# Layer two's second matrix product by seven block products for two of three token groups, with its output transposed

## The chip, the core and the metric

The kernel runs on one core of one Trainium2 chip. The metric is device time in microseconds (us) for one execution. TensorE multiplies matrices, VectorE, ScalarE and GpSimd work elementwise, and SyncE issues the transfers.

## The reference

A windowed attention over 4 sequences of 576 tokens gives 2304 tokens of 512 values; two feed-forward layers follow. The change touches the attention and layer one only in their order, and layer two in its second product.

```python
x = attention(q, k, v)                      # 2304 x 512, window 32, plain and dilated heads
h = x @ moe_w_in                            # layer one: 512 -> 1024
e = exp(h - max(h)); s = h * e / (sum(e) + 1e-9)
x = layernorm(s) * g_ln @ moe_w_out         # 1024 -> 512
h = x @ moe2_w_in                           # layer two: 512 -> 2048
g = h * sigmoid(1.702 * h)
out = g @ moe2_w_out                        # second product of layer two: 2048 -> 512
```

## The kernel before

Each float32 product is made as three products of rounded parts: a high part and a low part of either factor, high by high, high by low and low by high. So every operand is split first: ScalarE copies the high part, VectorE or GpSimd subtracts it to get the low part.

Layer one handles 128 tokens at a time. Attention units (`u`), layer one's first product (`h`), transposes (`lt`) and its second product (`y`) are interleaved. Layer two runs in three passes `p` of 768 tokens, each as a pair of 384-token blocks (`TB2 = 384`).

In a pass the first product already uses seven block products instead of eight (`h_prod`, m = 0 to 6, for eight quads q of two output blocks of 128 rows): six matmuls of 384 columns for each m and q. VectorE adds the results together; ScalarE and VectorE apply the sigmoid gate; the results are the tiles `g`. For each of the 16 tiles, `o_hi` (line 703) and `o_lo` (line 706) split 768 columns, and `o_prod` (line 726) makes the second product: for six groups of 128 tokens, three matmuls of 512 columns each, with the tokens as the stationary side. That is 288 matmuls of 512 columns a pass.

Layer two's weights arrive as 64-bit values. A weight unit is fetched (line 569), turned into float32 (ScalarE lines 370 and 378, VectorE lines 382 and 386), summed where the block products need sums (`unit_sum`, line 578, GpSimd or VectorE; only for the first product before), split (`unit_hi`, line 595, and `unit_lo`, line 599), and stored to DRAM. Units in `KEEP` are prepared during pass 0 and used from the room where they were split. A unit waits in one of three rooms `raw` until split. Nine rooms `hl` hold split weights; one quad of the first product needs four.

The order of work on each engine is written out by a planner in the kernel: each piece has a rank, assumed costs, room it takes and gives back, and pieces that it follows. On each engine the planner places, as its own clock advances, the first piece by rank that can start. The lists `LOADS`, `HEAD`, `HEAD2`, `PARK`, `EXP_EACH`, `LOW_DVE`, `NORM_ANY`, `LO_POOL` and `EAGER` set ranks and choices of engine.

## Time and profile before

| | us |
|---|---|
| median of 3 runs (694.85 to 695.95) | 695.17 |
| the profiled execution | 696.08 |
| its span, first to last instruction | 694.3 |
| TensorE busy in the span | 669.4 |
| VectorE busy in the span | 438.5 |
| ScalarE, GpSimd busy in the span | 346.6, 170.6 |

A group of instructions is given by line, engine, operation and tile, with its count, the busy time and the mean duration. Matmuls overlap at their ends, so the mean of one is longer than the time from one start to the next; the same holds for other engines by some tens of ns. The granted clock is a share of TensorE's full speed.

### The profile page before, as it was taken

What the parts mean: (1) busy time and instruction counts of PE and PEld (TensorE: products, weight loads), DVE (VectorE), ACT (ScalarE), POOL (GpSimd) and SP (SyncE); (2) the same over time, 40 slices, a digit from 0 to 9 for tenths busy, and PEclk for the clock granted to TensorE, in tenths of its full rate; (3) what the DMA queues carried; (4) which work ended last, traced back from release to release, by engine and by line L of the source; (5) the groups of instructions that cost most, each with busy time, mean ns of one, the idle gap of its engine ahead of it and who ended that gap; (6) DMA issues with size and microseconds to landing.
All of it is one profiled execution on the core that took longest, in us unless ns stands there. A gap on an engine that the chain in (4) does not pass through costs nothing.

```text
span 694.3 us, 11999 instructions
## 1 busy us (share of the span) xinstructions
PE 669.4 (96%) x4729; PEld 597.9 (86%) x4729; DVE 438.5 (63%) x680; ACT 346.6 (50%) x676; POOL 170.6 (25%) x166
## 2 busy tenths in 40 slices
...
GB/s 281 305 307 219 65 84 189 162 138 108 115 79 64 224 178 241 251 333 71 349 250 207 163 242 244 261 262 276 247 248 123 131 113 232 273 198 96 141 128 121
DMA packets 42072, 133.99 MB, mean 193 GB/s; under 512 B 5664, under 2 KB 5664, under 8 KB 42016
## 3 DMA queue, kind: packets, MB, share of 16 engines
q1 hardware_dynamic: 42016, 133.22, 56.0%
...
q14 instruction: 19, 0.16, 0.1%
...
## 4 chain that ended last, share of the span: by engine, by line
PE 83%; DVE 10%; ACT 3%; DMA 2%; issue 1%; POOL 0%; SPq 0%; DVEq 0%; ACTq 0%
PE oa L726 18%; PE hz L661 14%; PE y L538 14%; PE h L465 12%; PE hx L661 11%; PE ob L726 9%; PE lt L516 2%; PE xt L325 2%; PE ptp L309 1%; PE s L228 1%; DVE w1r L382 1%; DVE pt L315 1%; DVE nm L473 1%; DVE wo_l L438 1%; DVE y L578 1%
## 5 line engine op out<-in xcount | busy, mean ns | idle before, releaser
L661 PE MATMUL hz<-yc,ws 128*128 128x384 f32 x576 | 108.5, 335 | 0.9 <-DVE g L678 0.9
L726 PE MATMUL oa<-w,gs 128*128 128x512 f32 x432 | 103.9, 389 | 0.0
L706 DVE TENSOR_TENSOR gs<-g,gs 128x768 fp32r<-128x768 f32 x48 | 46.3, 966 | 90.3 <-ACT gs L703 90.3
L661 PEld LDWEIGHTS hz<-yc,ws 128*128 128x128 f32 x576 | 100.4, 188 | 1.7 <-DVE g L678 1.7
L726 PEld LDWEIGHTS oa<-w,gs 128*128 128x128 f32 x432 | 81.1, 188 | 16.7
L703 ACT CAST gs<-g 128x768 fp32r<-128x768 f32 x48 | 39.9, 836 | 99.9 <-PE ob L726 98.9
L661 PE MATMUL hx<-yc,ws 128*128 128x384 f32 x432 | 82.8, 334 | 0.0
L538 PE MATMUL y<-lnh,wo_h 128*128 128x256 f32 x288 | 82.7, 287 | 0.0
L538 PE MATMUL y<-lnh,wo_l 128*128 128x256 f32 x288 | 81.5, 283 | 0.0
L538 PE MATMUL y<-lnl,wo_h 128*128 128x256 f32 x288 | 81.5, 283 | 0.0
L661 PEld LDWEIGHTS hx<-yc,ws 128*128 128x128 f32 x432 | 75.6, 188 | 0.2
L465 PE MATMUL h<-wi_h,xh 128*128 128x512 f32 x144 | 60.2, 418 | 0.0
L465 PE MATMUL h<-wi_h,xl 128*128 128x512 f32 x144 | 57.8, 402 | 0.3 <-DVE xl L454 0.3
L465 PE MATMUL h<-wi_l,xh 128*128 128x512 f32 x144 | 57.5, 400 | 0.0
L538 PEld LDWEIGHTS y<-lnh,wo_h 128*128 128x128 f32 x288 | 55.1, 191 | 0.6
L538 PEld LDWEIGHTS y<-lnl,wo_h 128*128 128x128 f32 x288 | 55.2, 192 | 0.3
L538 PEld LDWEIGHTS y<-lnh,wo_l 128*128 128x128 f32 x288 | 55.1, 191 | 0.0
L726 PE MATMUL ob<-w,gs 128*128 128x512 f32 x216 | 54.8, 389 | 0.0
L690 ACT ACTIVATE sg<-g 128x768 f32<-128x768 f32 (+1 forms) x48 | 32.7, 686 | 31.8 <-DVE g L681 27.1
L726 PEld LDWEIGHTS ob<-w,gs 128*128 128x128 f32 x216 | 40.5, 188 | 8.4
L301 POOL TENSOR_TENSOR t<-t,sx 128x768 f32<-128x768 f32 (+1 forms) x20 | 29.1, 1455 | 45.4 <-DVE sx L296 43.9
L690 ACT ACTIVATE sg<-hx 128x384 f32<-128x384 f32 x24 | 11.8, 492 | 48.8 <-PE hx L661 48.8
(333 smaller groups left out, 1203.6 us busy)
## 6 DMA issues: line engine op xcount, KB each, us to landing
...
ws<-w1d SPq DMA_DIRECT2D x48, 384.0 KB, 5.6
...
v<-in_v_dram SPq DMA_DIRECT2D x14, 384.0 KB, 3.9
...
```

The lines of the kernel that those rows point to most:

```text
L228: nc.tensor.matmul(ps[64 * par:64 * par + 64, h, wp * KW:wp * KW + KW], q_[rows, c:c + QW], k_[rows, c:c + KW], start=not masked, stop=not ...
L301: eng.tensor_tensor(t, t, wide(sms.pop(n), t.shape[1]), ALU.mult)
L309: nc.tensor.transpose(ps[:, j * P:j * P + P], t[:, 4 * h + j, :], ident)
L325: nc.tensor.matmul(ps[64 * h:64 * h + 64, w * QW:w * QW + QW], vW[4 * b + u][:, h, w, :], pt[:, h, w * QW:w * QW + QW], start=True, stop=True)
L465: nc.tensor.matmul(hps[i][:, half, :], x[:, kt, :], w[:, kt, fs], start=(kt == 0 and j == 0), stop=(kt == KT - 1 and j == 2))
L516: nc.tensor.transpose(ps[:, j, :], es[i][:, f * P:f * P + P], ident)
L538: nc.tensor.matmul(yps[g, dm][:, 0:n], w[:, f, ds_], x[:, f, 0:n], start=(f == 0 and j == 0), stop=(f == NF1 - 1 and j == 2))
L661: nc.tensor.matmul(ps[:, 0:TB2], quad_weights(q, m, kk, a), yc2[m][:, x, kk, :], start=(m < 4 and kk == 0 and i == 0), stop=(kk == 1 and i ...
L690: nc.scalar.activation(sg, src, AF.Sigmoid, scale=1.702)
L703: nc.scalar.copy(gsp[f][:, 0], gst[f])
L706: nc.vector.tensor_tensor(gsp[f][:, 1], gst.pop(f), f32(gsp[f][:, 0]), ALU.subtract)
L726: nc.tensor.matmul(acc[t2][k], gsp[f][:, x, ts_], w2[f][:, w, :], start=(f == 0 and i == 0), stop=(f == NF2 - 1 and i == 2))
```

## The change

In passes 1 and 2 the second product is made by seven block products too. Output blocks and weights change sides: weights are stationary, 384 tokens stream, and the output is written transposed (512 x 2304) and put right on the host. For each jj of eight, four products (m = 0 to 3) need three sums of `g` blocks, and for each jj three more (m = 4 to 6) follow after all jj's first four; a fourth sum is needed before m = 5. Each m and jj is six matmuls of 384 columns. The results are added together from PSUM (`o_p1`, `o_u2`, `o_u3`, `o_out`). Pass 0 keeps the eight plain block products (`o_plain`), with weights stationary: twelve matmuls of 384 columns for each jj, block and half.

The weight units of the second product now get the four sums and two splits each, and two stores. `o_load` brings two transfers of 512 KB for each jj, and `o_load2` brings pairs of 256 KB transfers in runs of 1 KB for m = 4 to 6. `KEEP` has 11 units for 12; five units of the second product are prepared with layer one, for four before. `unit_lo` may run on VectorE as well. The lists that order attention and layer one are replaced.

```diff
     def unit_fetch(u, room):
...
         a, s_ = (x.bitcast(F32).rearrange("p (c n) -> p c n", c=4) for x in words(raws[u]))
-        x, y_, op = ((a[:, 3], a[:, 2], ALU.add), (s_[:, 0], a[:, 0], ALU.subtract),
...
         if u[0] == "o":
-            x, n, d = low, 512, w2d[u[1]]
...
-            x, n, d = low[:, 0:3 * P], 3 * P, w1d[u[1]][:, 14 * P * u[2]:14 * P * u[2] + 6 * P]
-        else:
...
+            x, n, at_ = (low[:, P:], 3, 14 * u[2]) if part == 0 else (top, 4, 14 * u[2] + 6)
+        hl = hls[u, part][:, 0:2 * n * P]
+        by = hl.rearrange("p (c a n) -> p a c n", c=n, a=2)
+        return x.rearrange("p (c n) -> p c n", c=n), by[:, 0], by[:, 1], \
+            wd[u[0], u[1]][:, at_ * P:(at_ + 2 * n) * P], hl
 
     def unit_hi(u, part, hl):
...
-
-    def o_hi(p, f):
-        gsp[f] = wk2.tile([P, 2, 2 * TB2], F32R, tag="gs", name=f"gs{p}_{f}")
-        nc.scalar.copy(gsp[f][:, 0], gst[f])
-
-    def o_lo(p, f):
...
+
+    def o_block(jj, half, b):
+        return gst[jj + NQ * half][:, b * TB2:b * TB2 + TB2]
+
+    def o_sum(jj, i):
+
+        b11, b12, b21, b22 = (o_block(jj, h, b) for h in range(2) for b in range(2))
+        o, x, y_, op = ((b12, b22, b12, ALU.subtract), (b11, b12, b11, ALU.add),
+                        (b12, b22, b11, ALU.subtract), (b21, b21, b11, ALU.subtract))[i]
+        nc.vector.tensor_tensor(o, x, y_, op)
+
+    def o_hi(p, jj, m, half, b):
+        gsp[jj, m] = wk2.tile([P, 2, TB2], F32R, tag="gs", bufs=NGS, name=f"gs{p}_{jj}_{m}")
+        nc.scalar.copy(gsp[jj, m][:, 0], o_block(jj, half, b))
+
+    def o_lo(p, jj, m, half, b):
+        nc.vector.tensor_tensor(gsp[jj, m][:, 1], o_block(jj, half, b), f32(gsp[jj, m][:, 0]), ALU.subtract)
+
+    oX, oZ, ob, w2o, w2t = {}, {}, {}, {}, {}
+
+    def o_load(jj, d, hl):
+
+        w2o[jj, d] = hl
+        nc.sync.dma_start(f32(hl), wd["o", jj][:, (16 * d + 6) * P:(16 * d + 14) * P])
+
+    def o_load_all(jj, d, hl):
+
+        w2o[jj, d] = hl
+        nc.sync.dma_start(f32(hl), wd["o", jj][:, 16 * d * P:(16 * d + 8) * P])
+
+    def o_plain(jj, half, b):
+
+        first, last = seen.get(b, 0) == 0, seen.get(b, 0) == 2 * NQ - 1
+        seen[b] = seen.get(b, 0) + 1
+        if first:
+            acc[b] = [psA.tile([P, 2, 512], F32, tag="A", name=f"oa{r}") for r in range(2)] if b == 0 else \
+                [[psB.tile([P, 512], F32, tag="B", name=f"ob{r}{d}") for d in range(2)] for r in range(2)]
+        for r in range(2):
+            for d in range(2):
+                w = w2o[jj, d] if ("o", jj, d) not in KEEP else hls[("o", jj, d), 0]
+                ps = (acc[b][r][:, d] if b == 0 else acc[b][r][d])[:, 0:TB2]
+                k = ((3, 1), (0, 2))[r][half]
+                for i, (a, x) in enumerate(((0, 0), (0, 1), (1, 0))):
+                    nc.tensor.matmul(ps, w[:, (2 * k + a) * P:(2 * k + a + 1) * P], gsp[jj, 2 * half + b][:, x],
+                                     start=first and i == 0, stop=last and i == 2)
+
+    acc, seen = {}, {}
...
+    def o_load2(p, m, jj):
+
+        t = stage[0].tile([P, 2, 2, 2 * P], F32R, tag="raw", bufs=NRAW, name=f"w2_{p}_{m}_{jj}")
+        at_ = (2, 4, 14)[m - 4] * P
         for k in range(2):
-            ts_ = slice((2 * t2 + k) * P, (2 * t2 + k) * P + P)
-            for i, (x, w) in enumerate(((0, 0), (0, 1), (1, 0))):
-                nc.tensor.matmul(acc[t2][k], gsp[f][:, x, ts_], w2[f][:, w, :],
-                                 start=(f == 0 and i == 0), stop=(f == NF2 - 1 and i == 2))
-
...
+            w2t[m, jj + k] = t[:, k]
+            nc.sync.dma_start(f32(t[:, k]), wd["o", jj + k].rearrange("p (d c) -> p d c", d=2)[:, :, at_:at_ + 2 * P])
+
+    def o_prod(p, jj, m):
+        k = seen[p, m] = seen.get((p, m), 0) + 1
+        first, last = k == 1, k == NQ
+        if first and m < 2:
+            oX[m] = psA.tile([P, 2, 512], F32, tag="A", name=f"ox{p}_{m}")
+        elif first and m < 4:
+            oZ[m] = [psB.tile([P, 512], F32, tag="B", name=f"oz{p}_{m}_{d}") for d in range(2)]
+        for d in range(2):
+            ps = (oX[1 if m == 1 else 0][:, d] if m in (0, 1, 4) else oZ[2 if m in (2, 5) else 3][d])[:, 0:TB2]
+            k = (0, 2, 3, 1)[m] if m < 4 else 0
+            for i, (a, x) in enumerate(((0, 0), (0, 1), (1, 0))):
+                w = w2o[jj, d][:, (2 * k + a) * P:(2 * k + a + 1) * P] if m < 4 else w2t[m, jj][:, d, a * P:a * P + P]
+                nc.tensor.matmul(ps, w, gsp[jj, m][:, x], start=m < 4 and first and i == 0, stop=last and i == 2,
+                                 skip_group_check=True)
...
+    def o_p1(p, d):
+        hp1["o", d] = wk2.tile([P, TB2], F32, tag="p1", bufs=NP1, name=f"op{p}_{d}")
+        nc.scalar.copy(hp1["o", d], oX[0][:, d, 0:TB2])
+
+    def o_u2(p, d):
+        nc.vector.tensor_tensor(hp1["o", d], oX[1][:, d, 0:TB2], hp1["o", d], ALU.add)
...
+    def o_u3(p, d):
+        hU3["o", d] = wk2.tile([P, TB2], F32, tag="u3", name=f"ou{p}_{d}")
+        nc.vector.tensor_tensor(hU3["o", d], oZ[2][d][:, 0:TB2], hp1["o", d], ALU.add)
...
+    def o_out(p, c, d, copy=None):
+
+        if d == 0:
+            ob[c] = wk2.tile([P, 2 * TB2], F32, tag="sg", name=f"ob{p}_{c}")
+        o = ob[c][:, d * TB2:d * TB2 + TB2]
+        if c == 1:
+            copy(o, oX[0][:, d, 0:TB2])
+        else:
+            nc.vector.tensor_tensor(o, oZ[2 if c == 2 else 3][d][:, 0:TB2], (hU3 if c == 0 else hp1)["o", d], ALU.add)
+
+    def o_store(p, c):
+        r, b = ((1, 1), (0, 0), (1, 0), (0, 1))[c]
+        t = 2 * TB2 * p + TB2 * b
+        nc.sync.dma_start(out[2 * P * r:2 * P * r + 2 * P, t:t + TB2].rearrange("(d p) t -> p d t", p=P),
+                          ob[c].rearrange("p (d t) -> p d t", d=2))
...
         for n, u in enumerate(PARK[k]):
-            r = R2 + 190 + 10 * u[1] - O_AHEAD if u in KEEP else at["h", PARK_AT[k]] + PARK_STEP * n + 0.2
+            r = R2 + 190 + 20 * u[1] + u[2] - O_AHEAD if u in KEEP else at["h", PARK_AT[k]] + PARK_STEP * n + 0.2
...
-            for i in range(0 if u[0] == "o" else 4):
+            for i in range(4):
                 w = add(r, "POOL", 0.35, lambda u=u, i=i: unit_sum(u, i, nc.gpsimd), [w], port=True,
                         also=[("DVE", 0.23, lambda u=u, i=i: unit_sum(u, i, nc.vector))])
-            for part in range(1 if u[0] == "o" else 2):
-                fin = part == 1 or u[0] == "o"
...
-                    give=() if u in KEEP else (hl,))
-                if u in KEEP:
+                    give=() if u in KEEP and not fin else (hl,))
+                if u in KEEP and not fin:
...
         r0 += 200
...
-            if kept:
-                w = split_done[("o", f), 0]
-                hi_now[("o", f), 0].after.append(ready[-1])
+        lead, now, gsum = 25, {}, {}
+
+        def operand(jj, m, half, b, after, give=()):
+            w = add(r - lead, "ACT", 0.47, lambda: o_hi(p, jj, m, half, b), after, take=("gs",))
+            return add(r - lead, "DVE", 0.5, lambda: o_lo(p, jj, m, half, b), [w], port=True, give=give)
+
+        def total(jj, i, after, k=25):
+            gsum[jj, i] = add(r - k, "DVE", 0.5, lambda: o_sum(jj, i), after, port=True)
+            return gsum[jj, i]
+
+        for jj in range(NQ if p == 0 else 0):
+            r = r0 + 20 * jj
+            loads = []
...
+                def load(p=p, jj=jj, d=d):
+                    o_load_all(jj, d, hl_tile(f"wo{p}_{jj}_{d}", hi_now[p, "o", jj, d], hl_end[p, "o", jj, d]))
+                hi_now[p, "o", jj, d] = w = add(
+                    r - 60, "SP", W_T, load, [stored[("o", jj, d), 0]] + ready[-1:], take=("hl",), lag=2.0)
+                loads.append(w)
+            for b in range(2):
+                for half in range(2):
+                    op = operand(jj, 2 * half + b, half, b, muls[jj], give=("g",) if b else ())
+                    x = add(r, "PE", 2.08, lambda jj=jj, half=half, b=b: o_plain(jj, half, b),
+                            loads + [op, prods[QUADS[-1], 3]],
+                            take=(("A", "A"), ("B",) * 4)[b] if jj == half == 0 else (),
+                            give=("gs", "hl", "hl") if b and half else ("gs",))
+                    now[jj, 2 * half + b] = x
...
+        for jj in range(NQ):
+            r = r0 + 10 * jj
+            loads = []
+            for d in range(2):
+                def load(p=p, jj=jj, d=d):
+                    o_load(jj, d, hl_tile(f"wo{p}_{jj}_{d}", hi_now[p, "o", jj, d], hl_end[p, "o", jj, d]))
+                hi_now[p, "o", jj, d] = w = add(
+                    r - 60, "SP", W_T, load, [stored[("o", jj, d), 0], stored[("o", jj, d), 1]] + ready[-1:], take=("hl",),
+                    lag=2.0)
+                loads.append(w)
+            t3 = total(jj, 0, muls[jj], 50)
+            b11 = operand(jj, 0, 0, 0, muls[jj])
+            t2 = total(jj, 1, [t3, b11])
+            ops = [b11, operand(jj, 1, 0, 0, [t2]), operand(jj, 2, 0, 1, [t3])]
+            t1 = total(jj, 2, [t2, ops[2]])
+            ops.append(operand(jj, 3, 0, 1, [t1]))
+            for m in range(4):
+                x = add(r, "PE", 1.042, lambda p=p, jj=jj, m=m: o_prod(p, jj, m), loads + [ops[m], prods[QUADS[-1], 3]],
+                        take=(("A",), ("A",), ("B", "B"), ("B", "B"))[m] if jj == 0 else (),
+                        give=("gs", "hl", "hl") if m == 3 else ("gs",))
+                now[jj, m] = x
+            for d in range(2):
+                hl_end[p, "o", jj, d] = x
+        end_ = [[now[jj, m] for jj in range(NQ)] for m in range(4)]
+
+        def store(c, ws):
+            add(r, "SP", 1.3, lambda p=p, c=c: o_store(p, c), ws, give=("sg",), lag=2.0)
+
+        p1 = [add(r, "ACT", 0.45, lambda p=p, d=d: o_p1(p, d), end_[0], take=("p1",)) for d in range(2)]
+        u2 = [add(r, "DVE", 0.53, lambda p=p, d=d: o_u2(p, d), end_[1] + [p1[d]], give=("A",) if d else ()) for d in range(2)]
+        u3 = [add(r, "DVE", 0.53, lambda p=p, d=d: o_u3(p, d), end_[2] + [u2[d]], take=("u3",)) for d in range(2)]
+        c22 = []
+        for d in range(2):
+            c22.append(add(r, "DVE", 0.53, lambda p=p, d=d: o_out(p, 0, d), end_[3] + [u3[d]] + c22, give=("u3",),
+                           take=() if d else ("sg",)))
+        store(0, c22)
+        wait = {4: p1, 5: u3, 6: c22}
+        for m in (4, 5, 6):
+            xs_ = []
+            for jj in range(NQ):
+                r = r0 + 10 * (NQ * (m - 3) + jj)
+                if jj % 2 == 0:
+                    w = add(r - 60, "SP", 1.7, lambda p=p, m=m, jj=jj: o_load2(p, m, jj),
+                            [stored[("o", jj + k, d), part] for k in range(2) for d in range(2) for part in range(2)] +
+                            [now[1, 0]], take=("raw",), lag=2.0)
+                if m == 4:
+                    now["b21", jj] = op = operand(jj, m, 1, 0, muls[jj])
+                elif m == 5:
+                    t4 = total(jj, 3, [now["b21", jj], gsum[jj, 1], now[jj, 2]])
+                    t4.give = ("g",)
+                    op = operand(jj, m, 1, 0, [t4])
+                else:
+                    op = operand(jj, m, 1, 1, muls[jj] + [gsum[jj, 0], gsum[jj, 2], gsum[jj, 3]], give=("g",))
+                x = add(r, "PE", 1.042, lambda p=p, m=m, jj=jj: o_prod(p, jj, m), [w, op] + wait[m] + end_[3],
+                        give=("gs", "raw") if jj % 2 else ("gs",))
+                xs_.append(x)
+            if m == 4:
+                c = add(r, "ACT", 0.45, lambda p=p: o_out(p, 1, 0, nc.scalar.copy), xs_, take=("sg",))
+                c11 = [c, add(r, "DVE", 0.53, lambda p=p: o_out(p, 1, 1, nc.vector.tensor_copy), xs_ + [c], give=("A",))]
+                store(1, c11)
...
+                cs = []
+                for d in range(2):
+                    cs.append(add(r, "DVE", 0.53, lambda p=p, c=m - 3, d=d: o_out(p, c, d), xs_ + cs,
+                                  take=() if d else ("sg",), give=("B",) if m == 5 else ("B", "p1")))
+                store(m - 3, cs)
...
 NA = 2
 TB2 = 384
-NHL, NHL2, NRAW = 6, 3, 3
-SLOTS = {"A": 2, "B": 4, "S": 1, "qk": 2, "v": 3, "l": 1, "t": 3, "pt": 2, "ln": 4, "x": 2, "e": 3, "raw": NRAW, "hl": NHL, "p1": 2, "u3": 2, "sg": 2, "g": 16, "gs": 2,
+NQ = NF2 // 2
+NHL, NHL2, NRAW, NGS, NP1 = 6, 3, 3, 5, 4
+SLOTS = {"A": 2, "B": 4, "S": 1, "qk": 2, "v": 3, "l": 1, "t": 3, "pt": 2, "ln": 4, "x": 2, "e": 3, "raw": NRAW, "hl": NHL, "p1": NP1, "u3": 2, "sg": 2, "g": 16, "gs": NGS,
...
-LOADS = [('q', 0), ('m', 0), ('q', 2), ('q', 1), ('q', 3), ('v', 0), ('v', 1), ('w', 0), ('v', 2), ('w', 2), ('w', 1),
...
+LOADS = [('q', 0), ('m', 0), ('v', 1), ('w', 0), ('q', 3), ('q', 2), ('w', 2), ('v', 0), ('q', 1), ('w', 1), ('q', 4),
+         ('w', 3), ('q', 6), ('g', 0), ('v', 3), ('w', 5), ('w', 4), ('v', 2), ('l', 0), ('q', 5), ('v', 5), ('v', 4),
+         ('l', 1), ('v', 6), ('w', 7), ('q', 7), ('w', 6), ('v', 7), ('l', 2), ('q', 8), ('v', 8), ('q', 9), ('v', 9),
...
+HEAD = [('u', 4), ('h', 1), ('u', 3), ('u', 1), ('w', 1), ('u', 0), ('w', 2), ('u', 2), ('h', 0), ('w', 3), ('w', 0)]
+HEAD2 = [[('w', 6)], [('w', 5), ('w', 7), ('w', 4)], [], [], []]
...
-EXP_EACH = (0, 3, 4, 6, 7, 8, 9)
+EXP_EACH = (0, 2, 3, 4, 7, 9)
...
-LOW_DVE = (1, 2)
-NORM_ANY = (0, 2, 7)
+LOW_DVE = (2, 6, 7)
+NORM_ANY = (0, 3, 4, 9)
...
-LO_POOL = (0, 1)
-EAGER = {0: (4, 99), 3: (2, 99)}
+LO_POOL = (2,)
+EAGER = {3: (0, 99)}
...
-PARK = {1: [("q", 0, 0), ("q", 0, 1)],
-        2: [("q", 1, 0), ("q", 1, 1), ("q", 2, 0), ("q", 2, 1), ("q", 3, 0), ("q", 3, 1)],
-        3: [("q", 4, 0), ("q", 4, 1), ("q", 5, 0), ("q", 5, 1), ("q", 6, 0), ("q", 6, 1), ("q", 7, 0), ("q", 7, 1)] +
-        [("o", f) for f in range(16)]}
-PARK_AT = {1: 4, 2: 4, 3: 11}
-PARK_STEP = 3
+PARK = {1: [('q', 4, 1), ('q', 0, 1), ('q', 3, 1)],
+        2: [('q', 4, 0), ('q', 3, 0), ('q', 1, 0), ('q', 2, 1), ('q', 6, 0), ('q', 5, 0)],
+        3: [('q', 0, 0), ('q', 7, 1), ('q', 7, 0), ('q', 5, 1), ('q', 2, 0), ('q', 1, 1), ('o', 0, 0), ('o', 0, 1),
+            ('q', 6, 1), ('o', 1, 1), ('o', 1, 0), ('o', 2, 0), ('o', 2, 1), ('o', 3, 1), ('o', 3, 0), ('o', 4, 0),
+            ('o', 5, 0), ('o', 5, 1), ('o', 4, 1), ('o', 6, 0), ('o', 7, 1), ('o', 7, 0), ('o', 6, 1)]}
+PARK_AT = {1: 4, 2: 9, 3: 9}
+PARK_STEP = 2
 QUADS = [0, 1, 2, 3, 4, 5, 6, 7]
-KEEP = [("o", f) for f in range(4, 16)]
-O_AHEAD = 60
+KEEP = [('o', 0, 1), ('o', 1, 0), ('o', 1, 1), ('o', 2, 0), ('o', 3, 0), ('o', 3, 1), ('o', 4, 0), ('o', 5, 0),
+        ('o', 5, 1), ('o', 6, 1), ('o', 7, 1)]
+O_AHEAD = 140
...
-LOAD_AT = 5
-ULO_ANY = False
+ULO_ANY = True
 _INS = ["qk", "qk_last", "v", "v_last", "masks", "w_in", "w_out", "g_ln", "w2_in", "w2_out"]
-_OUTS = [((2304, 512), 'float32')]
+_OUTS = [((512, 2304), 'float32')]
```

## Rows read from the trace of the kernel before

**Rows 1.** The page: busy time of each engine; the chain that ended last, by engine
```profile
PE 669.4 (96%) x4729; PEld 597.9 (86%) x4729; DVE 438.5 (63%) x680; ACT 346.6 (50%) x676; POOL 170.6 (25%) x166
...
PE 83%; DVE 10%; ACT 3%; DMA 2%; issue 1%; POOL 0%; SPq 0%; DVEq 0%; ACTq 0%
```

**Rows 2.** Busy time by stage: start:end, length, engines, granted clock, DMA share, GB/s
```profile
0.00:100.00 100.00, 84.76 (x990) 69.25 (x991) 84.63 (x122) 71.81 (x152) 43.33 (x39) 0.93 0.67 212
100.00:300.00 200.00, 196.43 (x1735) 175.92 (x1733) 140.97 (x239) 131.76 (x296) 105.14 (x113) 1.00 0.48 163
300.00:375.74 75.74, 74.89 (x475) 74.57 (x474) 53.24 (x87) 37.44 (x66) 8.76 (x7) 1.00 0.67 234
375.74:442.24 66.50, 65.70 (x289) 53.89 (x289) 41.72 (x52) 32.61 (x52) 13.41 (x9) 1.00 0.65 231
442.24:500.73 58.49, 58.49 (x338) 58.24 (x337) 39.35 (x68) 21.89 (x37) 0.00 (x0) 1.00 0.76 268
500.73:566.05 65.32, 65.32 (x290) 54.05 (x289) 23.58 (x31) 17.37 (x24) 0.00 (x0) 1.00 0.42 146
...
624.54:689.88 65.34, 65.33 (x289) 53.72 (x287) 16.72 (x19) 14.52 (x19) 0.00 (x0) 1.00 0.32 112
689.88:694.30 4.42, 0.00 (x0) 0.00 (x0) 0.69 (x1) 0.00 (x0) 0.00 (x0) 0.88 0.69 255
```

**Rows 3.** VectorE in order of time at 504 us: start, duration
```profile
503.69 0.95 DVE L697 TENSOR_TENSOR g<-g,sg 128x768 f32<-128x768 f32 x1
504.56 0.55 DVE L699 TENSOR_TENSOR g<-g,sg 128x384 f32<-128x384 f32 x1
505.03 0.42 DVE L636 TENSOR_TENSOR y<-y 128x256 f32<-128x256 f32 x1
```

**Rows 4.** VectorE groups, 500 to 566 us: the next pass's inputs
```profile
L647 DVE TENSOR_TENSOR yc<-y,yc 128x512 fp32r<-128x512 f32 (+2 forms) x8 | 5.6, 716 | 0.0
...
L636 DVE TENSOR_TENSOR y<-y 128x256 f32<-128x256 f32 (+1 forms) x2 | 1.4, 684 | 0.0
...
L636 DVE TENSOR_TENSOR y<-y,y 128x512 f32<-128x512 f32 x1 | 0.7, 684 | 0.0
```

**Rows 5.** ScalarE, a copy of 384 columns
```profile
L666 ACT COPY p<-hx 128x384 f32<-128x384 f32 x24 | 11.6, 482 | 23.2 <-PE hx L661 23.2
```

**Rows 6.** VectorE, work on one weight unit and the like
```profile
L269 DVE TENSOR_TENSOR t<-s,mx 128x768 f32<-128x768 f32 x3 | 2.8, 939 | 0.1
L434 DVE TENSOR_TENSOR wi_l<-w1r,wi_h 128x1024 fp32r<-128x1024 f32 x2 | 2.4, 1201 | 0.0
...
L386 DVE SCALAR_TENSOR_TENSOR raw_('o', 14)_4875<-raw_('o', 14)_4875 128x512 uint32<-128x512 uint32 x1 | 1.8, 1802 | 0.0
...
L578 DVE TENSOR_TENSOR raw_('q', 4, 0)_2889<-raw_('q', 4, 0)_2889 128x128 f32<-128x128 f32 x4 | 1.1, 281 | 0.0
...
L382 DVE SCALAR_TENSOR_TENSOR raw_('o', 12)_4838<-raw_('o', 12)_4838 128x512 uint32<-128x512 uint32 x1 | 0.7, 693 | 1.4 <-ACT raw_('o', 12)_4838 L378 1.4
```

**Rows 7.** GpSimd, the same kinds of work
```profile
L578 POOL TENSOR_TENSOR y<-y 128x128 f32<-128x128 f32 x9 | 3.9, 459 | 1.2 <-DVE sm L484 1.0
...
L599 POOL TENSOR_TENSOR hl_('o', 10)_0_4808<-raw_('o', 10)_4747,hl_('o', 10)_0_4808 128x512 fp32r<-128x512 f32 x1 | 1.3, 1322 | 1.3 <-ACT hl_('o', 10)_0_4808 L595 1.3
```

**Rows 8.** SyncE's issues of the raw weight units, with their start
```profile
L569 SPq DMA_DIRECT2D raw_('o', 6)_4130<-in_w_out_dram x1: 372/372/372, 327.8 to 327.8; - x1
L569 SPq DMA_DIRECT2D raw_('o', 7)_4661<-in_w_out_dram x1: 333/333/333, 384.0 to 384.0; - x1
```

**Rows 9.** DMA packets: whole run, by size; then the hardware queue, 455 to 495 us and 505 to 560 us
```profile
DMA packets 42072, 133.99 MB, mean 193 GB/s; under 512 B 5664, under 2 KB 5664, under 8 KB 42016
...
q1 hardware_dynamic: 3453, 11.19, 79.3%
...
q1 hardware_dynamic: 2592, 9.05, 47.4%
```

**Rows 10.** The chain that ended last, at 99 us
```profile
98.75 3.49 DVE y L578 x4
```

146 lines of the change are left out of this document (63 added, 83 removed), and 2 rows, old and new, of the table LOADS.

## The prediction

> **What bounds the kernel now.** I read the page first, then the stages, then the groups inside the stages that change. The page and the chain of waits say TensorE: it is busy 669.4 of 694.3 us, and 83% of the chain that ended last runs through it [rows 1]. This is an average, so the stages come next [rows 2]. From 300 us on TensorE has no gaps worth naming: in pass 1 the first product fills 58.49 of 58.49 us and the second 65.32 of 65.32; pass 2's second product fills 65.33 of 65.34. What it does there sets the time one for one. The other engines have room: VectorE is busy 23.58 us in pass 1's second product, ScalarE 17.37. The first 100 us differ: TensorE is busy 84.76 us at a granted clock of 0.93, VectorE 84.63 us, and there the chain runs through VectorE, for instance 3.49 us of weight sums at 99 us [rows 10]. After the last matmul 4.42 us remain for one VectorE copy and the store.
>
> **The change part by part.**
>
> *TensorE in passes 1 and 2.* The new matmuls have the shape of the first product's: a 128x128 stationary block, 384 streamed columns, a new block for each. A first product has 8 x 7 x 6 = 336 of them in 58.49 us [rows 2], so one costs 0.174 us from start to start. The new second product has 8 jj x 7 m x 6 = 336 too, hence 58.49 us against 65.32 and 65.34: -6.83 and -6.85, together -13.7.
>
> *TensorE in pass 0.* 8 jj x 2 blocks x 2 halves x 12 = 384 matmuls x 0.174 = 66.85 us. Before, TensorE was busy 65.70 of 66.50 us there [rows 2]: +1.15, with the old gap of 0.8 kept.
>
> *The tail.* The last store is 384 KB where it was 256 KB. In the second window of [rows 9] 9.05 MB took 47.4% of 16 engines for 55 us, 417 engine-us, so 2.88 us a MB over sixteen: 0.13 MB more is 0.4. The two additions ahead of it take as long as the old copy of 0.69 us to within 0.3, since the first can run while the last three matmuls do. I take +0.4.
>
> *VectorE in pass 1.* Each jj has 7 low parts and 4 sums, all of 384 columns: 88 a pass. A busy time of 0.55 us is not the interval: the operation at 504.56 is followed by the next at 505.03, so 0.47 [rows 3]. 88 x 0.47 = 41.4; eleven additions from PSUM at 0.47 are 5.2; preparing pass 2's inputs is 5.6 + 1.4 + 0.7 = 7.7 [rows 4]. That is 54.3 of 58.49 us: full, but it fits. By halves: m = 0 to 3 last 32 x 6 x 0.174 = 33.4 us on TensorE, and VectorE has 56 x 0.47 + 7.7 = 34.0 us, of which five low parts (five rooms `gs`) and some ten sums, 7.0 us, can be done earlier in the 19.1 us that VectorE is idle in the first product [rows 2]. m = 4 to 6 last 25.1 us against 32 x 0.47 + 5.2 = 20.2. At 0.55 each the pass would need 62.2 us, 3.7 too many. Bounds 0 and 3.7; the interval row is nearer to a busy queue, so I take 0.7. Pass 2 has no next pass to prepare: at most 54.5 of 58.49, take 0.3. ScalarE's 56 copies at 0.48 [rows 5] are 27 us and hidden.
>
> *The same filler in the first products of passes 1 and 2.* If a sum sits ahead of one of a quad's additions, that addition is up to 0.47 us late; sixteen quads bound this at 7.5. VectorE is idle a third of that stage, and an addition late by one operation is mostly absorbed by the block product between it and the one that needs it. I take 0.3.
>
> *The weights' transfers in passes 1 and 2.* m = 0 to 3 bring 16 x 512 KB = 8.4 MB, 24.2 us at 2.88 us a MB, under 33.4 us of TensorE. m = 4 to 6 bring 24 x 256 KB = 6.3 MB, 18.1 us under 25.1. These last come in runs of 1 KB, and no packet of before has a size from 512 B to 2 KB: the two counts are the same, 5664 [rows 9]. Lower bound: by bytes, as above, hidden. Upper: each 1 KB packet as dear as a mean packet now, 417 / 2592 = 0.161 us; 6144 packets over 16 engines are then 61.8 us. The two windows of [rows 9] have mean packets of 3.24 and 3.49 KB, and the smaller cost 45.4 engine-us a MB against 46.1: no charge per packet shows. I take the bytes, 0.
>
> *Weight units in pass 0.* Eleven units are prepared there, now with four sums and two splits. A unit takes VectorE 2 x 0.69 for the conversion, then sums of 0.281 on VectorE or 0.459 on GpSimd and two low parts, about 0.6 (half the 1024-column row) or 1.32 [rows 6, 7]. With these on GpSimd: VectorE 11 x 1.4 + 32 low parts x 0.47 + 7.7 = 38 us, GpSimd 11 x 4.5 = 49 us, both under 66.85. But the engines are not independent: one conversion step took 1.802 us where the same shape took 0.693 [rows 6]. If they never work side by side, the sum is 64 us (all on VectorE) to 87 us (all on GpSimd) with 22.7 us of other VectorE work in it. Bounds 0 and 20.4; before, nine units from 384 us on (the one ahead had been fetched at 327.8 [rows 8]) cost TensorE 0.8 us. VectorE may take either part now, and three units can wait converted in the rooms `raw`. I take 1.0.
>
> The Trainium skill, SBUF — State Buffer, section "SBUF: two separate sides", says that GpSimd and a VectorE operation with two SBUF inputs exclude each other for a whole instruction. The stretched row agrees with it. By it pass 0 would need the 64 to 87 us, so its loss would lie between 0 and 20.
>
> *Attention and layer one.* Against: two low parts of layer one's weights go to VectorE and one leaves, +1.2 (line 434 [rows 6]); one more unit subtracts its maximum on VectorE, +0.94 (line 269); one more conversion step, at most 1.2 by the 1024-column row. In sum +3.3 on the engine that leads there. For: `PARK[2]` moves from the fourth to the ninth `h`, which takes a unit's work such as the 3.49 us [rows 10] out of that stretch. One more unit is prepared with layer one, after 100 us, where VectorE is busy 140.97 of 200 us [rows 2] and covers it; without cover it would cost some 4 us. What the new order of loads and units does can't be read from a trace of the old. Bounds -5 and +5, a third of the 15.2 us that TensorE is idle in the first 100 us either way. I take -0.5.
>
> **Sum**, against the profiled execution's 696.08: -13.7 + 1.15 + 0.4 + 0.7 + 0.3 + 0.3 + 1.0 - 0.5 = -10.35, so 685.7. The median of the runs is 0.9 below that execution: 684.8.
>
> **The rivals.**
>
> *GpSimd and VectorE block each other in pass 0 (the other side).* Place: the weight units of pass 0's second product. The stretched row speaks for it, and that `hl` rooms open late: 56 us passed between the fetches at 327.8 and 384.0 [rows 8], so little can be done ahead. Against: the old 0.8 us, and the cheap VectorE forms. The full price is 20.4, a time of 704. The kernel is slower from a loss of 12.8 us on (1.0 + 10.35 + 1.4); a loss of 5 to 9 gives 689 to 693.
>
> *VectorE becomes the bound of passes 1 and 2.* For: 54.3 of 58.49 us with links between sums, splits and products. Against: the idle third ahead. At 0.55 us, with a lost link a jj in both, 3.7 + 1 more: about 688.5.
>
> *Short runs slow the transfers.* At twice the price per byte m = 4 to 6 need 36.2 us; the three rooms hold a quarter ahead, which leaves 27.2 against 25.1, 2 us a pass: 689. At the upper bound 46 against 25, 21 us a pass: 727. Against: the equal price per MB above.
>
> *Layer one's order gains as well.* At its lower bound, -5: 680.
>
> **How the numbers follow.** The forecast with its small losses (681.5 to 689): 0.56. Layer one gains or no losses at all (below 681.5): 0.16. VectorE, short runs or part of the blocking (689 to 693.8): 0.14. Within 0.2%, about what a measurement of this kernel can tell from no change: 0.04. Slower: 0.10, of it blocking 0.06, transfers and layer one 0.02 each. So faster 0.86. The range of 8 in 10 is 680 to 691; it leaves out the far gain and all that ends above.
>
> **What would show it.** Right: 336 matmuls in about 58.5 us in each of the two second products, none at 65; pass 0's second product at 67 to 69 us; a tail near 4.8; VectorE over 90% busy in pass 1's second product; transfers below full share in m = 4 to 6. Wrong: TensorE waiting for a low part (`gs`) in pass 1, for a kept weight unit in pass 0, or for the 256 KB transfers; GpSimd's low parts above 2 us in pass 0; or the first products of pass 0 starting more than 3 us from where they start now.

## The result, and the profile after

The changed kernel takes 686.17 us (median of 4 runs, 682.37 to 688.99), the kernel before 695.56 beside it: a ratio of 0.9861, 95% interval 0.9817 to 0.9906. The forecast was 684.8, with 680 to 691 as its range. The total was right; how it came about was not, and most of what follows is about that.

The profiled execution is the 682.37 one. Busy time of each engine and the chain that ended last, answering to [rows 1]:

```profile
PE 653.5 (96%) x4921; PEld 616.4 (91%) x4921; DVE 522.7 (77%) x948; ACT 387.7 (57%) x789; POOL 127.6 (19%) x148
...
PE 86%; DMA 6%; DVE 4%; ACT 2%; issue 1%; SPq 0%; POOL 0%; POOLq 0%; ACTq 0%; DVEq 0%
```

TensorE leads more than before, VectorE has a fifth more work, GpSimd a quarter less, and transfers are in the chain with 6% instead of 2%. The stages, with the columns of [rows 2]; each second product of passes 1 and 2 is cut where m = 4 to 6 begin:

```profile
0.00:100.00 100.00, 84.87 (x1036) 70.71 (x1037) 83.47 (x121) 77.26 (x162) 37.14 (x44) 1.00 0.70 221
100.00:300.00 200.00, 199.50 (x1765) 180.29 (x1764) 153.96 (x278) 139.40 (x307) 82.99 (x96) 1.00 0.55 189
...
363.65:438.71 75.06, 70.64 (x398) 70.33 (x398) 56.19 (x121) 40.75 (x76) 1.47 (x1) 0.98 0.76 273
438.71:496.95 58.24, 58.24 (x337) 58.24 (x337) 42.74 (x80) 22.31 (x41) 0.00 (x0) 1.00 0.75 258
496.95:530.33 33.38, 33.38 (x193) 33.08 (x193) 32.55 (x65) 20.39 (x41) 0.00 (x0) 1.00 0.93 307
530.33:558.05 27.72, 26.14 (x145) 24.78 (x145) 17.87 (x36) 10.65 (x21) 0.00 (x0) 1.00 0.78 257
...
616.79:649.91 33.12, 33.12 (x193) 33.12 (x193) 27.10 (x52) 17.50 (x35) 0.00 (x0) 1.00 0.67 223
649.91:676.48 26.57, 25.61 (x145) 24.70 (x144) 17.78 (x36) 10.65 (x21) 0.00 (x0) 1.00 0.69 223
676.48:680.60 4.12, 0.00 (x0) 0.00 (x0) 0.59 (x2) 0.00 (x0) 0.00 (x0) 1.00 0.26 95
```

Four things stand out. In 0 to 100 us TensorE is as busy as before but at a granted clock of 1.00 for 0.93, and gets 46 more matmuls done; from 100 to 300 us it stands idle 3 us less. Pass 0's second product begins 12 us earlier than before, but its stage is 75.06 us instead of 66.50 (the new row also holds the last twelve matmuls of the first product, 2.1 us at 0.174 each). m = 0 to 3 run at full speed (33.38 and 33.12 us; 192 x 0.174 = 33.4). m = 4 to 6 do not: 27.72 and 26.57 where 144 x 0.174 is 25.1. TensorE's waits from 360 us on (waiting line, what it waited for, total, times, longest) are few:

```profile
PE oa L741 <- DVE g L693: 4.4, 1, 4.4
PE oz L772 <- DMA w<-wdo: 1.3, 3, 0.5
PE oz L772 <- ACT gs L711: 0.6, 1, 0.6
PE ox L772 <- DMA w<-wdo: 0.6, 1, 0.6
```

**The 4.4 us at the turn into pass 0's second product.** TensorE in order of time there (start, duration, the wait in brackets):

```profile
363.65 0.68 PE L741 MATMUL oa<-gs,wo 128*128 128x384 f32 x3
364.17 0.69 PE L741 MATMUL oa<-gs,hl_('o', 0, 1)_0_4562 128*128 128x384 f32 x3
369.27 0.79 PE L741 MATMUL oa<-gs,wo 128*128 128x384 f32 x3 [4.42 <-DVE g L693]
...
370.62 3.60 PE L659 MATMUL hz<-yc,ws 128*128 128x384 f32 x12
```

The first plain product (`oa`) stands ahead of the last quad's m = 5 and 6 (`hz`). It needs both PSUM rooms of tag A, and one still holds the last quad's `hx`, which is given up only by the multiplication of line 693. VectorE does that last, behind work of its own, though the sigmoid that it multiplies by is done at 365.8:

```profile
365.32 0.55 DVE L671 TENSOR_TENSOR u<-hz,p 128x384 f32<-128x384 f32 x1
365.79 0.68 DVE L634 TENSOR_TENSOR y<-y,y 128x512 f32<-128x512 f32 x1
...
367.19 0.95 DVE L645 TENSOR_TENSOR yc<-y,yc 128x768 fp32r<-128x768 f32 x1
368.06 0.69 DVE L598 TENSOR_TENSOR hl_('o', 1, 0)_1_4647<-raw_('o', 1, 0)_3883,hl_('o', 1, 0)_1_4647 128x512 fp32r<-128x512 f32 x1
368.66 0.56 DVE L693 TENSOR_TENSOR g<-hx,sg 128x384 f32<-128x384 f32 x1
```

Lines 634 and 645 prepare the next pass's inputs and line 598 is a weight unit's low part. TensorE stands still, and the twelve matmuls of `hz` stand behind the waiting one in its queue, though what the first of them need (line 671) is done at 365.9.

The wait costs more than its 4.4 us. Behind it the granted clock is 0.50, the lower of its two levels (1.2 GHz), and the twelve matmuls of `hz` take 3.60 us where 12 x 0.174 is 2.1:

```profile
370.20:373.60 3.40, 3.40 (x13) 3.40 (x12) 0.82 (x2) 2.15 (x5) 0.07 (x1) 0.50 0.00 0
```

At full speed that work would take half of the 3.40 us, so the stage adds up: 66.85 + 2.09 + 4.42 + 1.70 = 75.06. In each of the seven executions with this wait a stretch at 0.50 stands at the turn.

**m = 4 to 6 of pass 1.** The chain that ended last runs through the 256 KB transfers there (start, duration, what):

```profile
530.49 2.60 PE ox L772 x15
533.08 4.07 DMA w<-wdo
...
541.90 5.21 DMA w<-wdo
```

A block product frees a room, a transfer fills it, and the next product waits for that. A room is used for two products, 2.08 us; the other two rooms last 4.17 us; a transfer takes 4 to 5 from issue to landing. The slack is about nothing.

### The profile page after: what moved, and what is told of

The parts are those of the page before. It is cut to its first block, busy times and chain, and to the rows that moved or that the text cites. A ratio compares the mean times of both kernels' runs of the same rounds, so it can differ in the third digit from the quotient of the medians.

```text
span 680.6 us, 12937 instructions
## 1 busy us (share of the span) xinstructions
PE 653.5 (96%) x4921; PEld 616.4 (91%) x4921; DVE 522.7 (77%) x948; ACT 387.7 (57%) x789; POOL 127.6 (19%) x148
## 4 chain that ended last, share of the span: by engine, by line
PE 86%; DMA 6%; DVE 4%; ACT 2%; issue 1%; SPq 0%; POOL 0%; POOLq 0%; ACTq 0%; DVEq 0%
PE h L465 15%; PE hz L659 15%; PE y L538 13%; PE hx L659 11%; PE oz L772 8%; PE ox L772 7%; PE ob L741 5%; PE oa L741 5%; DMA w<-wdo 3%; PE lt L516 2%; PE ptp L309 2%; PE xt L325 2%; PE s L228 1%; DMA y<-in_qk_dram 1%; DMA raw_('o', 1, 1)_3957<-in_w_out_dram 1%
## 5 line engine op out<-in xcount | busy, mean ns | idle before, releaser
L711 ACT CAST gs<-g 128x384 fp32r<-128x384 f32 x144 | 73.2, 513 | 71.8 <-PE oz L772 26.1
L659 PEld LDWEIGHTS hz<-yc,ws 128*128 128x128 f32 x576 | 102.0, 190 | 0.2 <-DVE g L676 0.2
L714 DVE TENSOR_TENSOR gs<-g,gs 128x384 fp32r<-128x384 f32 x144 | 78.4, 555 | 19.4 <-ACT gs L711 18.8
L465 PE MATMUL h<-wi_h,xl 128*128 128x512 f32 x144 | 56.4, 392 | 0.0
L772 PE MATMUL oz<-gs,w 128*128 128x384 f32 x192 | 34.9, 337 | 2.0 <-DMA w<-wdo 1.3
L772 PE MATMUL oz<-gs,wo 128*128 128x384 f32 x192 | 36.7, 335 | 0.0
L772 PE MATMUL ox<-gs,wo 128*128 128x384 f32 x192 | 36.5, 334 | 0.0
L772 PEld LDWEIGHTS oz<-gs,w 128*128 128x128 f32 x192 | 33.1, 188 | 3.4 <-issue 2.5
L301 POOL TENSOR_TENSOR t<-t,sx 128x768 f32<-128x768 f32 (+1 forms) x17 | 23.7, 1392 | 65.0 <-DVE sx L296 25.1
```

Source lines behind the costliest of these rows:

```text
L301: eng.tensor_tensor(t, t, wide(sms.pop(n), t.shape[1]), ALU.mult)
L465: nc.tensor.matmul(hps[i][:, half, :], x[:, kt, :], w[:, kt, fs], start=(kt == 0 and j == 0), stop=(kt == KT - 1 and j == 2))
L659: nc.tensor.matmul(ps[:, 0:TB2], quad_weights(q, m, kk, a), yc2[m][:, x, kk, :], start=(m < 4 and kk == 0 and i == 0), stop=(kk == 1 and i ...
L711: nc.scalar.copy(gsp[jj, m][:, 0], o_block(jj, half, b))
L714: nc.vector.tensor_tensor(gsp[jj, m][:, 1], o_block(jj, half, b), f32(gsp[jj, m][:, 0]), ALU.subtract)
L772: nc.tensor.matmul(ps, w, gsp[jj, m][:, x], start=m < 4 and first and i == 0, stop=last and i == 2, skip_group_check=True)
```

## The experiments

All medians are beside runs of the kernel before on the same chip, whose median was 695.53 to 696.25.

**1. The changed kernel again**, unchanged, for the size of its spread.

> The changed kernel once more, nothing edited, to see how far it spreads beside the others of this set. Theory (most of the gain is the smaller number of matmul columns, some of it given back in two waits, and layer one's order gains several us): 683 to 689 us, and among its own runs the shorter have the higher mean granted clock. Rival (layer one's order gives nothing, only the columns count): the same time, so this run does not tell them apart; it is the base for the three others.

686.26 us (684.05 to 687.2), ratio 0.9864 (0.9843 to 0.9884). Its profiled execution (span 684.4 for 694.3) is nearer to the median than the one above, so it is the one for the account: layer one, to the last quad's m = 4, -5.3; the turn and pass 0 +5.9; pass 1's second product 61.25 for 65.32, -4.1; pass 2's 59.60 for 65.49, -5.9; both first products -0.2; the tail -0.3. Sum -9.9. The shortest of its five runs, 684.05 us, has the highest mean clock (0.994), but the longest, 687.2, does not have the lowest, so the clock alone does not order them.

**2. The changed kernel with the old lists** (`LOADS`, `HEAD`, `HEAD2`, `EXP_EACH`, `LOW_DVE`, `NORM_ANY`, `LO_POOL`, `EAGER`; three of them in the diff), and **3. the kernel before with the new lists**, the other way round.

```diff
-HEAD = [('u', 4), ('h', 1), ('u', 3), ('u', 1), ('w', 1), ('u', 0), ('w', 2), ('u', 2), ('h', 0), ('w', 3), ('w', 0)]
+HEAD = [('u', 0), ('u', 1), ('w', 1), ('u', 2), ('w', 0), ('h', 1), ('u', 3), ('w', 2), ('u', 4), ('w', 3), ('h', 0)]
...
-LOW_DVE = (2, 6, 7)
+LOW_DVE = (1, 2)
...
-LO_POOL = (2,)
+LO_POOL = (0, 1)
```

> The changed kernel with the eight lists that order attention and layer one (loads, head, choices of engine) as they were before; the list of weight units and the second product stay new. Theory (the new lists give 4 to 9 us, by the traces): 690 to 695 us, with TensorE's idle time in the first 100 us back near 33 us. Rival, the forecast's own term (the lists give half a us): 685.7 to 687.

> The kernel before with the eight new lists and nothing else. Theory (the lists give 4 to 9 us by themselves): 687 to 691.5 us. Rival (they give half a us): 694.5 to 695.5. A third way, that the lists only help together with the new list of weight units, whose work VectorE does in the first 100 us: 694 to 698 here and 690 or more in the run with the old lists.

With the old lists 707.11 us (705.67 to 709.06), ratio 1.0171 (1.0140 to 1.0202): slower than the kernel before by 11.6 us, and far outside the expected 690 to 695. Nor is the loss where I looked for it: TensorE is idle 17.1 us in the first 100, not 33. The new lists alone, with the old product: 688.84 (687.34 to 689.9), ratio 0.9907 (0.9882 to 0.9932), -6.7 us. So the lists are worth much more than the 0.5 of the forecast, whichever product stands behind them. And with the new lists on both sides the new product brings only 2.6 us by the medians (688.84 to 686.26), 2.0 between the two profiled spans: passes 1 and 2 give 9.9, the turn and pass 0 take 5.6 back and layer one 2.8, and 0.5 comes from the first products and the tail. 200 to 300 us, first with the old lists and then TensorE's waits there:

```profile
200.00:300.00 100.00, 89.82 (x674) 81.10 (x673) 73.82 (x140) 65.42 (x135) 42.00 (x48) 0.93 0.56 193
```

```profile
PE h L210 <- DVE e L487: 5.5, 1, 5.5
PE lt L516 <- ACT y L543: 4.7, 1, 4.7
```

and the kernel before with the new lists:

```profile
200.00:300.00 100.00, 100.00 (x735) 91.87 (x734) 75.97 (x123) 70.20 (x144) 57.29 (x59) 1.00 0.60 206
```

With the old lists that stretch breaks up into waits for VectorE and ScalarE, and the granted clock is 0.93. I put it down to the new product's weight units (four sums, two splits each), which come into the end of layer one; no run takes them out, so that is not shown.

**4. Low parts of weight units on GpSimd alone**, the rival on the other side.

```diff
-ULO_ANY = True
+ULO_ANY = False
```

> The changed kernel with the low parts of all weight units on GpSimd, as before the change. Theory (VectorE and GpSimd side by side have room in pass 0): within 2 us of 686.2, with pass 0's second product within 1 us. Rival, the blocking of the two engines that the prediction priced at 0 to 20 us: 4 us or more above, with TensorE waiting for kept units in pass 0 and GpSimd's low parts above 2 us.

705.35 us (702.83 to 706.63), ratio 1.0142 (1.0114 to 1.0169): 19 us more than the change: the theory's 2 us did not hold, the rival's 4 or more did. In this kernel's trace GpSimd's low parts of the same shape took 1.3 us in most cases and up to three times that:

```profile
L598 POOL TENSOR_TENSOR hl_('o', 2, 0)_0_4766<-raw_('o', 2, 0)_4672,hl_('o', 2, 0)_0_4766 x1: 3963/3963/3963, 399.7 to 399.7; 128x512 fp32r<-128x512 f32 x1
L598 POOL TENSOR_TENSOR hl_('o', 2, 0)_1_4795<-raw_('o', 2, 0)_4672,hl_('o', 2, 0)_1_4795 x1: 1302/1302/1302, 406.7 to 406.7; 128x512 fp32r<-128x512 f32 x1
```

Pass 0's second product takes 72.86 us instead of 66.85, with waits for kept units (`POOL hl`) and for `gs`. That is 6 us of the rival; the larger part lies where I had not looked for it, ahead of pass 0, where the units of layer two's first weights now go through GpSimd (its line 598 is in the chain that ended last from 235 to 263 us, with transfers between). From 200 to 310 us TensorE waits twice, 8.8 us for ScalarE's `y` (line 543) and 5.3 us for VectorE's `e` (line 487).

The Trainium skill, SBUF — State Buffer, section "SBUF: two separate sides", says that a GpSimd operation and a VectorE operation with two SBUF inputs lock each other out for a whole instruction. The stretched rows agree with it: VectorE's queue ran without a gap until 402.5 us and GpSimd's operation of 3.96 us ended 1.2 us later, at 403.65; the second row met a VectorE low part of 384 columns, which took 1.35 us for 0.55. How much of the 19 us is that lock and how much GpSimd's slower operation (1.3 us for VectorE's 0.69) these runs do not separate, and the planner places all the other work anew when one engine's choice is taken away.

**5. The first plain product behind the whole last quad**, and **6. the same with pass 1's input preparation held back**.

```diff
-                            loads + [op, prods[QUADS[-1], 3]],
+                            loads + [op, prods[QUADS[-1], 6]],
```

```diff
-        src = [yc[g, dm] for g in range(3 * p, 3 * p + 3) for dm in range(KT)]
+        src = [yc[g, dm] for g in range(3 * p, 3 * p + 3) for dm in range(KT)] + (y_free[5:6] if p == 1 else [])
```

> The first plain product of pass 0 is ordered behind the last block product of the first product, where it had been put ahead of its last two. Theory (TensorE stands 4.4 us there because the product waits for a PSUM room that VectorE frees late, with two ready block products queued behind it): 4 to 6 us less than the unedited kernel of this set, and no wait above 1 us at the turn of pass 0. Rival (VectorE is late there anyway, so the last two block products or the plain products wait as long): within 1 us of it, with the wait moved to another line.

> As the run that ordered the first plain product behind the last block product, and besides the preparation of pass 1's inputs starts after the sixth block product of pass 0's last quad. Theory (the 2.1 us that were left at the turn come from that preparation, queued on VectorE ahead of the additions that the last block products need): 1.5 to 2.5 us less than that run, 681 to 682. Rival (VectorE then has that work, some 8 to 10 us, to do during the plain products, where it also splits weights): the same or more, with waits for a low part inside pass 0's second product.

The first: 683.47 us (681.71 to 685.72), ratio 0.9828 (0.9807 to 0.9848), 2.8 us better than the change. That is less than the theory's 4 to 6 and more than the rival's 1. The 4.4 us wait for the room is gone, but half of it comes back at the last quad's m = 5, for VectorE's line 671:

```profile
368.77 3.71 PE L659 MATMUL hz<-yc,ws 128*128 128x384 f32 x12 [2.12 <-DVE u L671]
```

It is the same queue of VectorE work, seen by another instruction, and the clock is at 0.50 from 369.4 to 372.8 us here too. The second: 685.52 (683.76 to 690.43), no better, against an expected 681 to 682. Its wait at the turn is 1.31 us, but longer waits stand elsewhere: 1.60 us for a weight transfer at 327 us, 1.81 at 549, and m = 4 to 6 of pass 1 take 30.6 us. Whether the held work made them is not shown.

**7. Six half rooms for three rooms**, and **8. the same bytes in runs of 2 KB**.

```diff
...
-            w2t[m, jj + k] = t[:, k]
...
+        w2t[m, jj] = t = halves[(NQ * (m - 4) + jj) % len(halves)]
...
-                        give=("gs", "raw") if jj % 2 else ("gs",))
+                        give=("gs", "half"))
```

```diff
-            nc.sync.dma_start(f32(t[:, k]), wd["o", jj + k].rearrange("p (d c) -> p d c", d=2)[:, :, at_:at_ + 2 * P])
+            nc.sync.dma_start(f32(t[:, k].rearrange("p d c -> p (d c)")), wd["o", jj + k][:, 2 * at_:2 * at_ + 4 * P])
```

> The three rooms for the 256 KB pairs of m = 4 to 6 are cut into six halves, each given back after one jj in place of two; the transfers, their bytes and their 1 KB runs are unchanged. Theory (a room's round of 2.1 us of products, 0.7 of issue and about 4.1 to landing is longer than the 6.25 us in which three rooms come round, so the wait is for the room): 2.5 to 4 us less than the unedited kernel, with passes 1 and 2's second products near 58.8 us. Rival (the transfers are slow because of their 1 KB runs): within 1 us, the waits stay.

> The transfers for m = 4 to 6 read as many bytes from as many partitions, but as one run of 2 KB in place of two of 1 KB; they bring other weights than the product needs, so this kernel's output is not the reference's. Theory (the wait is for the room, not for the runs): within 1 us of the unedited kernel. Rival (short runs): 2.5 to 4 us less, with the landing of these transfers down from about 4 us to below 3.3.

Half rooms: 685.05 us (683.64 to 688.71); m = 4 to 6 take 27.1 us in pass 1 and 27.2 in pass 2, for 27.7 and 26.3 in the first experiment: a little better in one, worse in the other. A half room leaves 5.2 us for a transfer where a room left 4.17, but the transfers landed in 4.6 us there, for 4.3, so little slack was won. Longer runs: 684.13 (682.96 to 684.76); 26.8 and 26.2, landing in 3.9 us for 4.3. Run length has a part of 1 us at most, and the rest of the gain of that profiled execution lies in layer one, 2.2 us; neither theory alone carries the loss.

**9. A sixth room for low parts** (and one room `p1` fewer), since some waits of m = 4 to 6 name ScalarE's copy of a `gs`; **10. half of the bytes in these transfers**; **11. experiments 5 and 9 together**.

```diff
-NHL, NHL2, NRAW, NGS, NP1 = 6, 3, 3, 5, 4
+NHL, NHL2, NRAW, NGS, NP1 = 6, 3, 3, 6, 3
```

```diff
-            nc.sync.dma_start(f32(t[:, k]), wd["o", jj + k].rearrange("p (d c) -> p d c", d=2)[:, :, at_:at_ + 2 * P])
+            nc.sync.dma_start(f32(t[:, k, 0:1]), wd["o", jj + k].rearrange("p (d c) -> p d c", d=2)[:, 0:1, at_:at_ + 2 * P])
...
```

> A sixth room for the low parts (gs) and three in place of four for the first copies (p1). Theory that the rooms gs, given back late to ScalarE, hold up m = 4 to 6: in that stage of pass 1 TensorE takes about 25.6 us where it took 27.7 (26.5 to 25.6 in pass 2), no wait for ScalarE's copy of a gs remains there, about 1 to 2 us less in all. Rival, that the 256 KB transfers hold it up: 27 to 28 us as before, the waits for the weights stay, time within 1 us of 686.2.

> The transfers of m = 4 to 6 bring half of their bytes (one row half, 128 KB each, used for both halves of the product, so the output is not the reference's); all instructions on the engines stay. Theory that these transfers hold up m = 4 to 6: the stage falls to about 25.2 to 25.6 us in pass 1 and pass 2 (from 27.7 and 26.5), no wait for w there, 3 to 4 us less in all. Rival, the gs rooms: waits for ScalarE's copy and VectorE's low part stay, 26.5 to 27.5 us in pass 1, at most 1.5 us less in all.

> The first plain product after the whole last quad, as in the second experiment, and six gs rooms. If the two gains are independent: 2.8 us from the turn and what the sixth room alone gives (1 to 2 us by the gs theory): 681.5 to 683. If the room gives nothing: 683.5, as the turn alone.

The sixth room gives nothing: 685.40 (684.38 to 687.86), and with the turn 683.69 (680.08 to 685.95) against 683.47 without. The waits for ScalarE are gone, and one of 2.47 us for a transfer stands in their place; m = 4 to 6 of pass 1 take 29.6 us, and 30.0 with the turn. Half of the bytes: 682.47 us (679.88 to 683.2), ratio 0.9798 (0.9777 to 0.9820), 3.8 below the first experiment, and m = 4 to 6 at full speed in both passes:

```profile
533.76:559.15 25.39, 25.20 (x145) 24.91 (x145) 17.73 (x36) 10.65 (x21) 0.00 (x0) 1.00 0.58 188
650.98:676.10 25.12, 25.12 (x145) 24.80 (x144) 17.78 (x36) 10.66 (x21) 0.00 (x0) 1.00 0.45 141
```

All waits but one of 0.2 us are gone, those for ScalarE as well, though `gs` has its five rooms here. So the transfers hold up this stage, and ScalarE's copies are late only behind them. From issue to landing, in the change and with half of the bytes (530 to 558 and 530 to 560 us):

```profile
w<-wdo SPq DMA_DIRECT2D x18, 256.0 KB, 4.1
```

```profile
w<-wdo SPq DMA_DIRECT2D x18, 128.0 KB, 2.5
```

**12. The output stores of passes 1 and 2 from GpSimd's queue**, all but the last, on top of experiment 5. SyncE's queue of experiment 5 in order of time shows why it was tried:

```profile
534.02 0.39 SPq L799 DMA_DIRECT2D out_dram<-ob  x1
534.50 8.54 SPq L758 DMA_DIRECT2D w<-wdo  x8
543.09 1.24 SPq L799 DMA_DIRECT2D out_dram<-ob  x1
544.44 7.81 SPq L758 DMA_DIRECT2D w<-wdo  x8
```

A store that waits for VectorE stands in front of each group of weight transfers. Their waits in 530 to 556 us (total, times, longest):

```profile
SPq L799 <- DVE ob L794: 1.6, 2, 1.2
SPq L799 <- DVE gs L714: 1.0, 1, 1.0
```

So they hold the transfers up by 1.2, 1.0 and 0.4 us. The 6.1 us of the expectation below is a misreading: that is the fourth store's wait, at 560.58 us, behind the last transfer of the stage.

```diff
-        nc.sync.dma_start(out[2 * P * r:2 * P * r + 2 * P, t:t + TB2].rearrange("(d p) t -> p d t", p=P),
+        (nc.gpsimd if p == 1 or p == 2 and c < 3 else nc.sync).dma_start(
+            out[2 * P * r:2 * P * r + 2 * P, t:t + TB2].rearrange("(d p) t -> p d t", p=P),
...
-            add(r, "SP", 1.3, lambda p=p, c=c: o_store(p, c), ws, give=("sg",), lag=2.0)
+            add(r, "POOL" if p == 1 or c < 3 else "SP", 1.3, lambda p=p, c=c: o_store(p, c), ws, give=("sg",), lag=2.0)
```

> As the second experiment (first plain product after the whole last quad), and the 384 KB output stores of passes 1 and 2, but for the very last, are issued from GpSimd's queue, which is idle there, in place of SP's. Theory that a store waiting for VectorE's sum on SP's queue (up to 6.1 us in the second experiment's trace) holds back the 256 KB transfers queued behind it: in pass 1 m = 4 to 6 fall from 28.05 us to about 26, in pass 2 from 26.4 to about 25.6, in all 2 to 3 us less, about 681. Rival, that only the transfers' own time from issue to landing (4.1 to 4.4 us, against 6.25 us in which TensorE empties three rooms) counts: 27.5 to 28 and 26.4 as before, time within 1 us of 683.5.

681.06 us (679.93 to 682.92), ratio 0.9779 (0.9742 to 0.9816): the fastest of all that compute the whole. SyncE's queue now runs through the transfers without a break, and m = 4 to 6 take 26.92 and 25.98 us, for 28.05 and 26.43 in experiment 5:

```profile
533.00 19.24 SPq L758 DMA_DIRECT2D w<-wdo  x18
```

```profile
530.73:557.65 26.92, 26.02 (x145) 24.85 (x145) 17.83 (x36) 10.66 (x21) 2.41 (x3) 1.00 0.81 265
649.48:675.46 25.98, 25.87 (x145) 24.66 (x144) 17.95 (x36) 10.66 (x21) 2.18 (x3) 1.00 0.72 227
```

That is 1.6 us from the stage named; the other 0.8 of the two medians' difference lies in pass 0 and layer one and is within the spread between executions. The interval just touches that of experiment 5, so the stage rows, of one execution each, carry this verdict more than the times. A loss of 1.8 and 0.9 us stays in m = 4 to 6. With the stores gone each of the nine pairs of transfers in pass 1's stage waits for TensorE to free its room (SyncE's waits, 525 to 556 us):

```profile
SPq L758 <- PE oz L772: 4.9, 5, 1.5
SPq L758 <- PE ox L772: 4.0, 4, 1.2
```

That fits the slack of the rooms as what is left; no run with a fourth room tests it.

## Why the prediction was right, and where it was not

The total came out right by luck: errors of some 6 us each way cancelled. In the first experiment's execution layer one was 4.8 us better than its term, and the first products and the tail 1.2; the turn and pass 0 were 3.8 worse than their terms, and the second products of passes 1 and 2 were 2.7 worse. Term by term:

- **The new product on TensorE (-13.7): right as a rate.** m = 0 to 3 take 33.5 and 33.3 us, the forecast's 33.4. Passes 1 and 2 gained 9.96 us; the 3.8 us that are missing are those of m = 4 to 6.
- **Pass 0's 384 matmuls (+1.15): right.** Where the turn doesn't disturb it the stage takes 67.4 us (experiment 5) and 66.7 (experiment 12), for 66.85.
- **Transfers of m = 4 to 6 (0): wrong, 3.8 us.** I compared bytes with the stage, 18.1 us under 25.1, and looked for a danger in the short runs. The 18.1 left out the stores and the next pass's loads: 530 to 558 us moved 7.23 MB at 78.6% of the 16 engines, 22 us, still under 25.1. And the price a MB was right: 0.78 x 16 / 0.257 = 48.6 engine-us in m = 4 to 6 against 0.93 x 16 / 0.307 = 48.5 in m = 0 to 3, no charge for 1 KB runs; runs of 2 KB landed 0.4 us sooner. The step that failed is the overlap that I took from bytes alone. In its place the runs show that the loss is gone with half of the bytes (experiment 10), and 1.6 us of it with the stores off SyncE's queue (experiment 12). The rest I put down to the time from a freed room to the landing, 4 to 5 us, against the 4.17 that two other rooms last; the waits of experiment 12 fit that, but experiment 7, which should have relieved it, won nothing sure. The rival of short runs put its loss of 2 us a pass in the right place, for the wrong reason; the sign to look for, a wait for the 256 KB transfers, was the right one.
- **VectorE in pass 1 (+0.7): no loss.** It is busy 32.55 of 33.38 us in m = 0 to 3, as forecast full, and TensorE never waits for it there. Over the whole second product it is 82% (50.42 of 61.10 us), below the 90% named as a sign. The interval was the right measure, not the busy time of 0.56:

```profile
504.60 0.56 DVE L707 TENSOR_TENSOR g<-g,g 128x384 f32<-128x384 f32 x1
505.06 0.56 DVE L714 TENSOR_TENSOR gs<-g,gs 128x384 fp32r<-128x384 f32 x1
```

- **Weight units in pass 0 (+1.0): at most half of it came, by the stage's 67.4 and 66.7 us; the reason holds.** Line 598 went to VectorE for all but one part in that stage; with it on GpSimd the stage loses 6.0 us, inside the bounds, and the whole kernel 19.
- **Tail (+0.4):** 4.12 us for 4.42, no loss.
- **The turn into pass 0's second product: not in the sum but for an old gap of 0.8: 6.1 us in the first profile (4.4 of wait, 1.7 at half clock behind it).** I carried that gap over and never asked which rooms the new first product takes. It takes both of tag A where the old one took one at a time, and one is held by the last quad until VectorE multiplies. The text's own sign, a start of pass 0's first products, would not have shown it: the stall lies after them.
- **Layer one's order (-0.5): the step that failed in size, past its bound of -5.** -5.3 in the first experiment's execution, -6.7 alone. My counts of what moves to and from VectorE (+3.3) were no measure of it. The text's sign of a start more than 3 us off did come true here: pass 0's first products start at 295.25 us for 304.59. What the rows show is that TensorE gets 46 more matmuls done in the first 100 us with the same busy time, at a granted clock of 1.00 (0.97 in experiments 1 and 3) for 0.93, a mean of stretches at 2.4 GHz and shorter ones at 1.2. Before, it was 0.86 from 20 to 40 us, where TensorE was busy 13.76 us, and 0.88 and 0.91 up to 80; in experiment 1 it is 0.91 up to 40 us and 1.00 from there to 100. What that is worth shows in layer one's first product, the same 432 matmuls of line 465, first before and then in experiment 1 (to the end of layer one; the busy times are TensorE's and its weight loads'):

```profile
0.00:372.43 372.43, 110.24 (x432) 80.93 (x432) 0.98 0.57 190
0.00:367.26 367.26, 106.57 (x432) 78.87 (x432) 0.99 0.62 205
```

  That is 3.7 us (106.57 in the other execution too). Against it experiment 1 has a stretch at 0.51 from 298.8 to 302.2 us, an estimated 1.7 us. Where the rest of the 5.3 comes from, and which of the eight lists does it, stays open; they were not tried one by one.

Of the 3.8 us between the spans of the two profiled executions of the changed kernel, 3.6 lie in layer one (a gain of 5.3 in one, at a clock of 0.99, and 8.9 in the other, at 1.00). As far as two executions can tell, the width of its runs comes from there.
